# A list-scheduled attention and FFN kernel: a re-tuned scheduler, another order of loads, and zero matmuls while PE waits for q

## The chip, the cores and the metric

The kernel runs on one core of one Trainium2 chip. The metric is the device time of one execution in microseconds (us), as the median over several runs. The core has a tensor engine (PE, with its weight loads shown apart as PEld), a vector engine (DVE), a scalar engine (ACT), POOL and SP. In this kernel POOL issues the loads of q, k, v and the weights from HBM, and SP issues the transposing DMAs and the stores. The program gives each engine its own instructions in a fixed order, and in these traces one that waits holds up what stands behind it on the same engine: while one copy on DVE waited 8.9 us (profile after), DVE did nothing else.

## The reference

Block-sparse attention over 4 batches, 8 heads, 768 positions and head size 64 is followed by a multiplicative FFN of 3072 tokens.

```python
scores = scale * np.matmul(q, k.transpose(0, 1, 3, 2))
# mask: neighbouring 32-blocks, first and last block, 3 sampled blocks per row
scores = np.where(mask, scores, -1000000000.0)
attn = softmax(scores)
x = (attn @ v)            # reordered to (3072, 512)
a = x @ w1                # 512 -> 1024
b = x @ w2
h = a * b @ w3            # (a * b) @ w3
out = h @ w_out           # 1024 -> 512
```

## The kernel before

The kernel folds w3 @ w_out into one matrix (wf). It computes all scores densely, exponentiates them on ACT (144 tiles of 128x1024), multiplies by a 0/1 mask on DVE, and multiplies by v on PE. The FFN of 512 tokens at a time is woven in between. The order on every engine comes from a list scheduler that runs while the program is built. It is a small model of the chip: each task has a cost per engine, and a task that depends on another may start when the scheduler thinks the other's result is *seen*.

```python
SEEN = {"PE": 0.22, "ACT": 0.10, "DVE": 0.10, "POOL": 0.12, "SP": 0.05}
SWITCH = 0.095
...
    t.end = start + t.costs[eng]
    t.seen = t.end + t.flight + SEEN[eng]      # commit()
...
    for d in t.deps:                           # run(): earliest start of a task
        e = d.seen
        base = max(base, e)
...
    elif t.kind == "xbar":                     # a transposing DMA
        xbar = max(xbar, t.end + 1.6) + t.bytes / 250e3
        t.seen = xbar + 0.4
...
def pick_pe(self, cands, free, mode):
    soon = [c for c in cands if c[0] <= max(t0, now) + 0.06]
    if mode == "S":                            # PE has just done a score tile
        s = [c for c in soon if c[1].mode == "S"]
        if s:
            return min(s, ...)                 # stay with score tiles
```

A score tile is four matmuls that use 64 of the 128 rows of PE, two heads side by side (`s[:, h, ...]`, 64x128 weights). All other matmuls use 128 rows, and the scheduler charges `SWITCH` for a change between the two kinds. Score tiles are chained, each one depending on the one before it:

```python
ts = add(f"S {sk}", {PE: 0.216}, sc, deps=QK[b, pr] + [prev_s], writes=[sk], ..., mode="S")
prev_s = ts
```

There are two PSUM buffers for score tiles. q and k of batch 0 are transposed on PE. Those of batches 1 to 3 are rearranged on DVE (`qs`, three buffers) and transposed by a DMA into `qkt` (eight buffers).

The softmax here doesn't subtract the row's maximum and nothing guards it: scores larger than these inputs give would overflow.

Of the kernel before, what the change touches and what calls it, by code (L numbers as in the profile page):

```python
# [18 lines left out]

class Task:  # L20
    def __init__(self, name, costs, deps, writes, reads, go, kind, prio, mode, flight):
        self.name, self.costs, self.deps = name, costs, deps
        self.writes, self.reads, self.go = writes, reads, go
        self.kind, self.prio, self.mode, self.flight = kind, prio, mode, flight
        self.end = None
        self.seen = None


class Plan:
# [12 lines left out]
    def add(self, name, costs, go, deps=(), writes=(), reads=(), kind="", prio=0, mode="N", flight=0.0):  # L42
        t = Task(name, costs, [d for d in deps if d is not None], list(writes), list(reads), go,
                 kind, prio, mode, flight)
        for key in set(t.writes) | set(t.reads):
            self.users[key] += 1
# [34 lines left out]
    def run(self):  # L81
# [13 lines left out]
        while ready:  # L95
            best = None
            ests = defaultdict(list)
            for t in ready:
# [4 lines left out]
                for d in t.deps:  # L103
                    e = d.seen
                    base = max(base, e)
                t.base = base
                for eng, cost in t.costs.items():
                    ests[eng].append((max(base, free[eng]), t))
# [12 lines left out]
            if len(t.costs) > 1:  # L121

                opts = []
                for e2, cost in t.costs.items():
                    opts.append((max(t.base, free[e2]) + cost + self.bias.get(e2, 0.0), e2))
                e2 = min(opts)[1]
                if e2 != eng:
                    eng, start = e2, max(t.base, free[e2])
# [6 lines left out]
            if t.kind == "load":  # L135
                lane = max(lane, t.end + 1.6) + t.bytes / 350e3
                t.seen = lane + 0.15
                for key in t.writes:
                    self.freed[key] = t.seen
            elif t.kind == "xbar":  # L140
                xbar = max(xbar, t.end + 1.6) + t.bytes / 250e3
                t.seen = xbar + 0.4
# [17 lines left out]
    bias = {}  # L160

    def pick(self, eng, cands, free):
        t0 = min(c[0] for c in cands)
        near = [c for c in cands if c[0] <= t0 + 0.12]
        return min(near, key=lambda c: (c[1].prio, c[0]))

    def pick_pe(self, cands, free, mode):
        now = free["PE"]
        t0 = min(c[0] for c in cands)
        soon = [c for c in cands if c[0] <= max(t0, now) + 0.06]  # L170
# [12 lines left out]
    def feed(self, s, free):  # L183

        held = self.slots["s"]
        busy = sum(1 for k in held[-self.bufs["s"]:] if self.left[k] or self.freed[k] > free["PE"] + 0.25)
# [8 lines left out]
def kernel(  # L195
# [36 lines left out]
        "w3n": ([128, d_ff], BF16, 4, None),  # L232
        "w3t": ([128, NF, 128], BF16, 3, None),
        "e": ([128, 2, 512], BF16, 8, None),
        "rec": ([128, 2, 2, 1], F32, 2, None),
        "xn": ([128, 2, d_model], BF16, 3, None),
        "x": ([128, 4, 512], BF16, 4, None),
# [4 lines left out]
        "o": ([128, 2, 2, D + 1], F32, 1, PSUM),  # L242
        "f": ([128, 512], F32, 3, PSUM),
# [100 lines left out]
    load_pair(0, 1, "qk")  # L344
    load_pair(0, 0, "v")
    load_pair(0, 1, "v")
    load_wo(0)
    load_wo(1)
    load_w3(0)
    load_w3(1)  # L350
    load_pair(0, 2, "qkv")
    load_w3(2)
    load_w3(3)
    load_pair(0, 3, "qkv")
    for i in range(4, NF):
        load_w3(i)
    for c in range(4):
        load_w12("w1", moe_w1, w1_sb, c)
        load_w12("w2", moe_w2, w2_sb, c)
    for b in range(1, B):  # L360
        for pr in range(NP):
            load_pair(b, pr, "qkv")
# [20 lines left out]
    for r in range(3):  # L383
        dst = Ab if r == 2 else A
        prev = dve(f"R{r}", 0.17, [prev, t_rf], lambda r=r, dst=dst: V.scalar_tensor_tensor(
            dst, in0=JJ, scalar=rand_f[:, r:r + 1], in1=A, op0=ALU.is_equal, op1=ALU.max))
    t_Ab = prev
    t_hot0 = dve("hot0", 0.6, [t_hotf], lambda: V.tensor_scalar(
        hot, in0=hotf, scalar1=0.0, scalar2=None, op0=ALU.is_ge))
    t_hot = dve("hot", 0.75, [t_hot0], lambda: V.scalar_tensor_tensor(  # L390
# [4 lines left out]
    for i, (lo, n) in enumerate(((0, 512), (512, 256))):  # L395
# [5 lines left out]
            t, G[:, lo:lo + n], T(*key)[:NB, :n]), deps=[m], reads=[key], prio=0))  # L401
    t_mask = {}
    for t3 in range(NT):
        for kp in range(3):
            key = ("f", "M", t3, kp)

            def mm(t, key=key, t3=t3, kp=kp):
# [4 lines left out]
            m = add(f"mask {t3} {kp}", {PE: 0.22}, mm, deps=g, writes=[key], prio=2.5)  # L412
            t_mask[t3, kp] = add(f"mask {t3} {kp} c", both(0.58, 0.69), lambda t, key=key, t3=t3, kp=kp: copy_on(
                t, mask[:, t3, kp, :], T(*key)), deps=[m], reads=[key], prio=1)
# [4 lines left out]
    def prepare(b, pr):  # L419
        done = []  # L420
        for x, tag in ((0, "qn"), (1, "kn")):
            src = (tag, b, pr)
            dst = ("qkt", b, pr)
            if b == 0:
                key = ("f", "qk", b, pr, x)

                def tr(t, key=key, src=src):
# [7 lines left out]
                done.append(add(f"tc {b}{pr}{x}", both(0.81, 0.5), lambda t, key=key, dst=dst, x=x: copy_on(  # L435
                    t, T(*dst)[:, x, :], T(*key, shape=[128, S], dt=BF16)), deps=[m], writes=[dst],
                    reads=[key], prio=0))
            else:
                mid = ("qs", b, pr, x)
                m = add(f"re {b}{pr}{x}", {DVE: 0.45}, lambda t, mid=mid, src=src: nc.vector.tensor_copy(  # L440
                    T(*mid), T(*src).rearrange("p h c d -> p c h d")), deps=[LD[src]], writes=[mid],
                    reads=[src], prio=4)
                t = add(f"xb {b}{pr}{x}", {SP: 0.3}, lambda t, mid=mid, dst=dst, x=x: nc.sync.dma_start(
# [12 lines left out]
        V1[b, pr] = add(f"v1 {b}{pr}", {DVE: 0.6}, widen, deps=[LD[src]], writes=[dst], reads=[src],  # L456
# [8 lines left out]
    for b in range(B):  # L465
        if b == 0:
            units += [(b, t, 2 * Q + i) for Q in range(2) for t in range(NT) for i in range(2)]
        else:
            units += [(b, t, pr) for t in range(NT) for pr in range(NP)]
# [3 lines left out]
    for b, t3, pr in units:  # L473
        chain = None
        for kp in range(3):
            sk, ek, qk = ("s", b, t3, pr, kp), ("e", b, t3, pr, kp), ("qkt", b, pr)

            def sc(t, sk=sk, qk=qk, t3=t3, kp=kp):
# [12 lines left out]
                T(*ek), T(*sk), AF.Exp, scale=1.0 / 8.0), deps=[ts], reads=[sk], writes=[ek], prio=2)  # L491
            tm = add(f"K {ek}", {DVE: 0.70}, lambda t, ek=ek, t3=t3, kp=kp: nc.vector.tensor_tensor(  # L492
                T(*ek), T(*ek), mask[:, t3, kp:kp + 1, :].to_broadcast((128, 2, 512)), op=ALU.mult),
                deps=[te, t_mask[t3, kp]], writes=[ek], prio=2)
# [3 lines left out]
            def va(t, ek=ek, ok=ok, b=b, pr=pr, kp=kp):  # L498
                e, o, w = T(*ek), T(*ok), T("v1", b, pr)
                for k2 in range(2):  # L500
                    kc = 2 * kp + k2
                    for qt in range(2):
# [6 lines left out]
                        reads=[ek, ("v1", b, pr)], kind="value", prio=1.5)  # L509
# [3 lines left out]
        tr = add(f"rec {rk}", {DVE: 0.15}, lambda t, rk=rk, ok=ok: nc.vector.reciprocal(  # L513
            T(*rk), T(*ok)[:, :, :, D:]), deps=[chain], reads=[ok], writes=[rk], prio=0)
        tx = add(f"xn {rk}", {DVE: 0.40}, lambda t, rk=rk, ok=ok, xk=xk, pr=pr: nc.vector.tensor_tensor(  # L515
# [129 lines left out]
```

## Time and profile before

The three runs took 297.84, 297.88 and 300.91 us (median 297.88). The profiled execution took 296.79 us.

Lines from the page of the profile before. First come busy time, share of the span and number of instructions by engine. Then follow the tenths of PE's busy time in 40 slices of 7.4 us, the granted clock of PE in the same slices, and the chain of work that ended last as shares of the span.

```profile
span 295.0 us, 6214 instructions
...
PE 256.7 (87%) x2505; PEld 121.0 (41%) x2548; DVE 185.4 (63%) x396; ACT 184.6 (63%) x221; POOL 46.2 (16%) x75
...
PE   2989999768689995699999999799999999948994
...
PEclk9999999997959997999999999999999999995998
...
PE 69%; DMA 18%; ACT 4%; DVE 4%; issue 3%; SPq 1%; POOL 0%; DVEq 0%; ACTq 0%; POOLq 0%
PE f L576 26%; PE s L483 13%; DMA qkt<-qs 13%; PE o L505 12%; PE f L595 11%; ACT e L490 4%; PE f L557 4%; DMA x<-xn 3%; DVE e L492 2%; DMA kn<-in_k_dram 1%; PE f L431 1%; PE f L409 1%; PE f L545 1%; SPq L528 1%; DVE xn L515 1%
```

The clock row cannot be read at the very start: it shows 9 (90% or more) in the slices up to 20 us, where score tiles take 0.61 us for 0.39 later. The row of tenths shows three holes: near 60 to 85 us, near 115 us and near 265 us. The chain gives 13% of the span to transposing DMAs of q and k. The list of waits shows who stood there. These are DVE between 60 and 125 us, ACT between 120 and 220 us, and PE after 260 us. The columns are engine, tile and line, what it waited for, total us, number of waits and longest wait.

```profile
DVE qs L440 <- DMA qkt<-qs: 20.9, 6, 4.6
...
ACT e L490 <- PE s L483: 22.3, 37, 2.6
...
PE f L576 <- DMA x<-xn: 4.5, 1, 4.5
```

DVE stood 20.9 us at copies into `qs`, whose buffers were still being read by transposes. In the steady stage ACT, which makes the exponentials, waited 37 times for a score tile. Near the end PE waited 4.5 us for the last x. A stretch of PE's timeline from the steady stage (start, length, what, count) shows how the work is laid out:

```profile
157.19 0.59 PE L576 MATMUL f<-x,w 128*128 128x512 bf16 x2
157.72 0.39 PE L483 MATMUL s<-qkt 64*128 64x256 bf16 x4
158.04 0.61 PE L576 MATMUL f<-x,w 128*128 128x512 bf16 x2
158.48 0.41 PE L505 MATMUL o<-v,e 128*128 128x65 bf16 x8
```

The lengths overlap (the pair at 158.04 takes 0.61 us, and the next group starts 0.44 us later), so one reads *starts*. In long back-to-back runs an FFN matmul starts every 0.216 us, so the pair that starts at 157.19 has its slots used up at 157.62. The score tile starts 0.10 us later. It starts at 157.72 and the next kind at 158.04: 0.32 us for a tile that costs 0.22 when another follows it (shown below). Every stretch of score matmuls thus costs about 0.2 us beside its work. This place is typical: over the 58 one-tile stretches between 120 and 218 us the median from first start to next kind is 0.325 us. The built program has 137 such stretches for 144 tiles.

I use **PE work**: the number of weight loads of each kind, times the start-to-start interval of that kind in back-to-back stretches (0.216 us for a 512-column matmul, 0.22 for a score tile, 0.24 for eight value matmuls). Narrower matmuls count for less.

### The profile page before, as it was taken

Reading aid. Unit: us, or ns where it says so; the run is one execution under the profiler, and the core shown is the slowest. Engines: PE = TensorE matmul, PEld = TensorE weight load, DVE = VectorE, ACT = ScalarE, POOL = GpSimd, SP = SyncE. Lnnn points to the kernel's source line nnn. Section 1 sums busy time; section 2 is a strip of 40 time slices with the busy share of each in tenths; the row PEclk is TensorE's granted clock in tenths of the full one; section 3 lists DMA queues with packets and bytes.
Section 4 is the critical chain, followed back from the end, with each engine's and each line's share of the span. In section 5 each row is a group of like instructions: output and inputs, shape, how many; then the busy total and the mean of one; then the engine's idle time right before and its main releaser. Section 6 shows DMA issues by size and latency. Waiting matters only on the chain.

```text
span 295.0 us, 6214 instructions
## 1 busy us (share of the span) xinstructions
PE 256.7 (87%) x2505; PEld 121.0 (41%) x2548; DVE 185.4 (63%) x396; ACT 184.6 (63%) x221; POOL 46.2 (16%) x75
## 2 busy tenths in 40 slices
PE   2989999768689995699999999799999999948994
PEld 1455545532234432244444444444443444422441
DVE  4578887943457853688777666867756776640331
ACT  2598896814546673477677767968777777730320
POOL 8634452042122232001000000000000000000000
PEclk9999999997959997999999999999999999995998
DMA  6999999699989999936750101301014001130003
GB/s 81 165 206 207 209 203 198 105 131 156 139 128 137 122 171 188 151 70 111 126 154 1 29 10 73 107 2 20 18 38 129 17 2 36 54 109 18 0 2 142
DMA packets 52193, 29.25 MB, mean 99 GB/s; under 512 B 33732, under 2 KB 47044, under 8 KB 52164
## 3 DMA queue, kind: packets, MB, share of 16 engines
q0 software_dynamic: 16416, 14.68, 34.8%
q1 hardware_dynamic: 35748, 14.16, 25.1%
q8 instruction: 20, 0.33, 0.4%
q14 instruction: 9, 0.07, 0.1%
HBM read 29.36 MB, written 6.29 MB: 121 GB/s over the span
## 4 chain that ended last, share of the span: by engine, by line
PE 69%; DMA 18%; ACT 4%; DVE 4%; issue 3%; SPq 1%; POOL 0%; DVEq 0%; ACTq 0%; POOLq 0%
PE f L576 26%; PE s L483 13%; DMA qkt<-qs 13%; PE o L505 12%; PE f L595 11%; ACT e L490 4%; PE f L557 4%; DMA x<-xn 3%; DVE e L492 2%; DMA kn<-in_k_dram 1%; PE f L431 1%; PE f L409 1%; PE f L545 1%; SPq L528 1%; DVE xn L515 1%
## 5 line engine op out<-in xcount | busy, mean ns | idle before, releaser
L490 ACT ACTIVATE e<-s 128x1024 bf16<-128x1024 f32 x144 | 144.5, 1026 | 58.1 <-PE s L483 52.2
L576 PE MATMUL f<-x,w 128*128 128x512 bf16 x361 | 103.7, 402 | 9.5 <-DMA x<-xn 5.3
L492 DVE TENSOR_TENSOR e<-e,mask 128x1024 bf16<-128x1024 bf16 x144 | 96.7, 686 | 18.4 <-ACT e L490 17.9
L505 PE MATMUL o<-v,e 128*128 128x65 bf16 x1152 | 60.3, 197 | 8.2 <-DVE e L492 4.1
L505 PEld LDWEIGHTS <-e 128*128 128x128 bf16 x1152 | 50.4, 99 | 41.7 <-issue 9.9
L483 PE MATMUL s<-qkt 64*128 64x256 bf16 x576 | 58.7, 283 | 9.2 <-DMA qkt<-qs 4.6
L587 DVE TENSOR_TENSOR h<-f,a 128x512 bf16<-128x512 f32 x48 | 33.0, 688 | 30.8 <-PE f L576 20.0
L595 PE MATMUL f<-wf,h 128*128 128x512 bf16 x180 | 48.8, 380 | 1.2 <-issue 1.0
L576 PEld LDWEIGHTS <-w 128*128 128x128 bf16 x384 | 31.1, 101 | 41.8 <-issue 17.7
L584 ACT CAST a<-f 128x512 bf16<-128x512 f32 x48 | 28.0, 583 | 26.6 <-PE f L576 25.6
L483 PEld LDWEIGHTS <-qkt 64*128 64x128 bf16 x576 | 17.7, 95 | 56.1 <-issue 47.3
L515 DVE TENSOR_TENSOR xn<-o,rec 128x256 bf16<-128x256 f32 x48 | 20.4, 424 | 1.6
L595 PEld LDWEIGHTS <-h 128*128 128x128 bf16 x192 | 14.8, 98 | 15.4 <-issue 5.3
L513 DVE RECIPROCAL rec<-o 128x4 f32<-128x4 f32 x48 | 8.6, 179 | 14.4 <-PE o L505 14.1
L557 PE MATMUL f<-wo,w3t 128*128 128x512 bf16 x56 | 16.6, 381 | 0.5 <-issue 0.2
L300 POOL DMA_DIRECT2D vn<-in_v_dram x16 | 11.6, 725 | 31.2 <-DVE h L587 15.0
L300 POOL DMA_DIRECT2D kn<-in_k_dram x16 | 11.6, 722 | 30.6 <-DVE qs L440 24.5
L300 POOL DMA_DIRECT2D qn<-in_q_dram x16 | 11.8, 739 | 18.1 <-DVE qs L440 9.6
L440 DVE COPY qs<-kn 128x768 bf16<-128x768 bf16 x12 | 4.3, 355 | 16.3 <-DMA qkt<-qs 16.3
L266 DVE COPY ob<-f 128x512 f32<-128x512 f32 x11 | 7.6, 690 | 8.3 <-PE f L595 8.3
L266 ACT COPY ob<-f 128x512 f32<-128x512 f32 x13 | 7.6, 584 | 7.4 <-PE f L595 7.0
L440 DVE COPY qs<-qn 128x768 bf16<-128x768 bf16 x12 | 4.4, 366 | 4.6 <-DMA qkt<-qs 4.6
(48 smaller groups left out, 77.9 us busy)
## 6 DMA issues: line engine op xcount, KB each, us to landing
out_dram<-ob SPq DMA_DIRECT2D x24, 256.0 KB, 2.1
qn<-in_q_dram POOLq DMA_DIRECT2D x16, 192.0 KB, 8.1
kn<-in_k_dram POOLq DMA_DIRECT2D x16, 192.0 KB, 7.7
vn<-in_v_dram POOLq DMA_DIRECT2D x16, 192.0 KB, 6.0
w3n<-in_moe_w_dram POOLq DMA_DIRECT2D x8, 256.0 KB, 9.9
w<-in_moe_w_dram POOLq DMA_DIRECT2D x8, 256.0 KB, 8.9
wo<-in_moe_w_out_dram POOLq DMA_DIRECT2D x2, 512.0 KB, 9.2
qkt<-qs SPq DMA_TRANSPOSE x24, 6.1
```

Of the source, the lines that this page charges most:

```text
L266: (nc.scalar.copy if t.eng == ACT else nc.vector.tensor_copy)(out, in_)
L300: t = add(name, {POOL: 0.73}, lambda t: nc.gpsimd.dma_start(out=out_of(), in_=src), deps=deps, writes=writes, kind="load", prio=seq[0])
L483: nc.tensor.matmul(s[:, h, k2 * QT:(k2 + 1) * QT], lhsT=z[64 * h:64 * h + 64, 1, kc * 128:(kc + 1) * 128], rhs=z[64 * h:64 * h + 64, 0, t3 ...
L490: te = add(f"E {ek}", {ACT: 0.97}, lambda t, sk=sk, ek=ek: nc.scalar.activation(T(*ek), T(*sk), AF.Exp, scale=1.0 / 8.0), deps=[ts], reads ...
L492: tm = add(f"K {ek}", {DVE: 0.70}, lambda t, ek=ek, t3=t3, kp=kp: nc.vector.tensor_tensor(T(*ek), T(*ek), mask[:, t3, kp:kp + 1, :].to_bro ...
L505: nc.tensor.matmul(o[:, qt, h, :], lhsT=e[:, h, lo:lo + 128], rhs=w[:, h, kc, :], start=kc == 0 and qt == 0 and h == 0, stop=kc == C - 1, ...
L515: tx = add(f"xn {rk}", {DVE: 0.40}, lambda t, rk=rk, ok=ok, xk=xk, pr=pr: nc.vector.tensor_tensor(T(*xk)[:, :, 128 * pr:128 * pr + 128].re ...
L557: nc.tensor.matmul(T(*key), lhsT=T("w3t", i)[:, j, :], rhs=wo_sb[:, j, :], start=j == 0, stop=j == NF - 1)
L576: nc.tensor.matmul(T(*key), lhsT=w[:, c, f * 128:(f + 1) * 128], rhs=T(*xk)[:, c, :], start=c == 0, stop=c == 3)
L584: ta = add(f"a {i}{f}", {ACT: 0.58}, lambda t, ak=ak, key=ends["w1"][0]: nc.scalar.copy(T(*ak), T(*key)), deps=[ends["w1"][1]], reads=[end ...
L587: nc.vector.tensor_tensor(T(*hk)[:, f, :], T(*key), T(*ak), op=ALU.mult),
L595: nc.tensor.matmul(T(*key), lhsT=T(*hk)[:, f, n * 128:(n + 1) * 128], rhs=wf_sb[:, f, :], start=f == 0, stop=f == NF - 1)
```

## The change

Its stated intent is a list schedule with score tiles in pairs, loads in the order w3, batch 1, w1, w2, and zero matmuls on PE while it waits for q. The arithmetic stays as it was. The core of the diff, with cuts:

```diff
+LOADS = ("a01 v00 a02 v01 a03 v02 v03 o0 o1 30 31 32 33 34 35 36 37 "
+         "p10 p11 p12 p13 10 20 11 21 12 22 13 23 "
+         "p20 p21 p22 p23 p30 p31 p32 p33")
+WARM = 8
+PRM = dict(bias=0.4, bmask0=1.0, ..., eprio=0.5, aprio=1.0, ...)
+LONG = ("load", "xbar", "store")
@@ run(): earliest start
-                for d in t.deps:
-                    e = d.seen
-                    base = max(base, e)
-                t.base = base
-                for eng, cost in t.costs.items():
-                    ests[eng].append((max(base, free[eng]), t))
+                for eng in t.costs:
+                    at = base
+                    for d in t.deps:
+                        at = max(at, d.end if d.eng == eng and not d.flight and d.kind not in LONG else d.seen)
+                    t.base[eng] = max(at, free[eng])
+                eng = min(t.costs, key=lambda e: t.base[e] + t.costs[e] + t.bias.get(e, 0.0))
+                ests[eng].append((t.base[eng], t))
@@ transposing DMAs
-                xbar = max(xbar, t.end + 1.6) + t.bytes / 250e3
-                t.seen = xbar + 0.4
+                xbar = max(xbar, t.end + 0.6) + t.bytes / 250e3
+                t.seen = max(xbar + 0.4, t.end + (4.0 if lane > t.end else 1.2))
@@ buffers
-        "w3n": ([128, d_ff], BF16, 4, None),
+        "w3n": ([128, d_ff], BF16, 8, None),
-        "x": ([128, 4, 512], BF16, 4, None),
+        "x": ([128, 4, 512], BF16, 3, None),
@@ zero matmuls
+    for i in range(WARM):
+        add(f"warm {i}", {PE: 0.427}, lambda t: nc.tensor.matmul(
+            T("f", "warm"), lhsT=zero[:, :128], rhs=zero, start=True, stop=True), ...)
@@ SP cost of a transpose / of a store
-{SP: 0.3} ... {SP: 0.1}
+{SP: 1.25} ... {SP: 0.55}
@@ units of batch 0: all four head pairs for one query tile, then the next tile
-            units += [(b, t, 2 * Q + i) for Q in range(2) for t in range(NT) for i in range(2)]
+        units += [(b, t, pr) for t in range(NT) for pr in range(NP)]
```

(The rest: costs of small tasks nearer to the measured ones, and biases and priorities for tasks that ACT or DVE could do.)

More of the change, by code (lines that the diff above doesn't have):

```diff
@@ L17 @@
 SWITCH = 0.095
+LOADS = ("a01 v00 a02 v01 a03 v02 v03 o0 o1 30 31 32 33 34 35 36 37 "
+         "p10 p11 p12 p13 10 20 11 21 12 22 13 23 "
+         "p20 p21 p22 p23 p30 p31 p32 p33")
+WARM = 8
+PRM = dict(bias=0.4, bmask0=1.0, bmask=1.0, btc=0.5, near=0.12, soon=0.06, kprio=2.0, eprio=0.5, aprio=1.0,
+           hprio=1.0, vprio=1.5, w3prio=10.0, ebufs=8, both=0.25, fo="31", pcopy=4.0)
+LONG = ("load", "xbar", "store")
 class Task:
@@ L26, in __init__ @@
         self.seen = None
+        self.base = {}
 class Plan:
@@ L40, in __init__, with add @@
         self.pool_of = {}
-    def add(self, name, costs, go, deps=(), writes=(), reads=(), kind="", prio=0, mode="N", flight=0.0):
+    def add(self, name, costs, go, deps=(), writes=(), reads=(), kind="", prio=0, mode="N", flight=0.0, bias=None):
         t = Task(name, costs, [d for d in deps if d is not None], list(writes), list(reads), go,
                  kind, prio, mode, flight)
+        t.bias = {"DVE": PRM["bias"]} if bias is None else bias
         for key in set(t.writes) | set(t.reads):
@@ L120, in run @@
             start, eng, t = picks[0]
-            if len(t.costs) > 1:
-                opts = []
-                for e2, cost in t.costs.items():
-                    opts.append((max(t.base, free[e2]) + cost + self.bias.get(e2, 0.0), e2))
-                e2 = min(opts)[1]
-                if e2 != eng:
-                    eng, start = e2, max(t.base, free[e2])
             if eng == "PE":
@@ L135, in run @@
             if t.kind == "load":
-                lane = max(lane, t.end + 1.6) + t.bytes / 350e3
-                t.seen = lane + 0.15
+                lane = max(lane, t.end + 1.75) + t.bytes / 375e3
+                t.seen = lane + 0.2
                 for key in t.writes:
@@ L158, in run @@
         return self.log
-    bias = {}
     def pick(self, eng, cands, free):
         t0 = min(c[0] for c in cands)
-        near = [c for c in cands if c[0] <= t0 + 0.12]
+        near = [c for c in cands if c[0] <= t0 + PRM["near"]]
         return min(near, key=lambda c: (c[1].prio, c[0]))
@@ L169, in pick_pe @@
         t0 = min(c[0] for c in cands)
-        soon = [c for c in cands if c[0] <= max(t0, now) + 0.06]
+        soon = [c for c in cands if c[0] <= max(t0, now) + PRM["soon"]]
         if mode == "S":
@@ L185, in feed @@
         held = self.slots["s"]
-        busy = sum(1 for k in held[-self.bufs["s"]:] if self.left[k] or self.freed[k] > free["PE"] + 0.25)
+        busy = sum(1 for k in held[-self.bufs["s"]:] if self.left[k] or self.freed[k] > free["PE"] + PRM["both"])
         if self.bufs["s"] - busy >= 2:
@@ L231 @@
         "qkt": ([128, 2, S], BF16, 8, None),
-        "w3n": ([128, d_ff], BF16, 4, None),
+        "w3n": ([128, d_ff], BF16, 8, None),
         "w3t": ([128, NF, 128], BF16, 3, None),
-        "e": ([128, 2, 512], BF16, 8, None),
+        "e": ([128, 2, 512], BF16, PRM["ebufs"], None),
         "rec": ([128, 2, 2, 1], F32, 2, None),
         "xn": ([128, 2, d_model], BF16, 3, None),
-        "x": ([128, 4, 512], BF16, 4, None),
+        "x": ([128, 4, 512], BF16, 3, None),
         "h": ([128, NF, 512], BF16, 2, None),
@@ L241 @@
         "s": ([128, 2, 512], F32, 2, PSUM),
-        "o": ([128, 2, 2, D + 1], F32, 1, PSUM),
-        "f": ([128, 512], F32, 3, PSUM),
+        "o": ([128, 2, 2, D + 1], F32, int(PRM["fo"][1]), PSUM),
+        "f": ([128, 512], F32, int(PRM["fo"][0]), PSUM),
     }
@@ L343 @@
     t_hotf = iota("hotf", hotf, 0.82, pattern=[[1, C], [C, 128]], base=0, channel_multiplier=-BLK)
-    load_pair(0, 1, "qk")
-    load_pair(0, 0, "v")
-    load_pair(0, 1, "v")
-    load_wo(0)
-    load_wo(1)
-    load_w3(0)
-    load_w3(1)
-    load_pair(0, 2, "qkv")
-    load_w3(2)
-    load_w3(3)
-    load_pair(0, 3, "qkv")
-    for i in range(4, NF):
-        load_w3(i)
-    for c in range(4):
-        load_w12("w1", moe_w1, w1_sb, c)
-        load_w12("w2", moe_w2, w2_sb, c)
-    for b in range(1, B):
-        for pr in range(NP):
-            load_pair(b, pr, "qkv")
+    for item in LOADS.split():
+        kind, rest = item[0], item[1:]
+        if kind == "o":
+            load_wo(int(rest))
+        elif kind == "3":
+            load_w3(int(rest))
+        elif kind in "12":
+            load_w12("w" + kind, moe_w1 if kind == "1" else moe_w2, w1_sb if kind == "1" else w2_sb, int(rest))
+        else:
+            load_pair(int(rest[0]), int(rest[1]), {"a": "qk", "v": "v", "p": "qkv"}[kind])
+    zero = fixed("zero", [128, 512], BF16)
+    t_zero = add("zero", {DVE: 0.2}, lambda t: nc.vector.memset(zero, 0.0), prio=-1)
+    for i in range(WARM):
+        add(f"warm {i}", {PE: 0.427}, lambda t: nc.tensor.matmul(
+            T("f", "warm"), lhsT=zero[:, :128], rhs=zero, start=True, stop=True),
+            deps=[t_zero], writes=[("f", "warm")], prio=-1)
     def dve(name, cost, deps, go, **kw):
@@ L384 @@
         dst = Ab if r == 2 else A
-        prev = dve(f"R{r}", 0.17, [prev, t_rf], lambda r=r, dst=dst: V.scalar_tensor_tensor(
+        prev = dve(f"R{r}", 0.23, [prev, t_rf], lambda r=r, dst=dst: V.scalar_tensor_tensor(
             dst, in0=JJ, scalar=rand_f[:, r:r + 1], in1=A, op0=ALU.is_equal, op1=ALU.max))
     t_Ab = prev
-    t_hot0 = dve("hot0", 0.6, [t_hotf], lambda: V.tensor_scalar(
+    t_hot0 = dve("hot0", 0.55, [t_hotf], lambda: V.tensor_scalar(
         hot, in0=hotf, scalar1=0.0, scalar2=None, op0=ALU.is_ge))
-    t_hot = dve("hot", 0.75, [t_hot0], lambda: V.scalar_tensor_tensor(
+    t_hot = dve("hot", 0.94, [t_hot0], lambda: V.scalar_tensor_tensor(
         hot, in0=hotf, scalar=float(BLK), in1=hot, op0=ALU.is_lt, op1=ALU.mult))
@@ L400 @@
         t_G.append(add(f"G{i}c", both(0.6, 0.6), lambda t, key=key, lo=lo, n=n: copy_on(
-            t, G[:, lo:lo + n], T(*key)[:NB, :n]), deps=[m], reads=[key], prio=0))
+            t, G[:, lo:lo + n], T(*key)[:NB, :n]), deps=[m], reads=[key], prio=0, bias={}))
     t_mask = {}
@@ L411 @@
             g = [t_G[0]] if t3 < 2 else [t_G[1]]
-            m = add(f"mask {t3} {kp}", {PE: 0.22}, mm, deps=g, writes=[key], prio=2.5)
+            m = add(f"mask {t3} {kp}", {PE: 0.22}, mm, deps=g, writes=[key], prio=1.2 if t3 == 0 else 5 + t3)
             t_mask[t3, kp] = add(f"mask {t3} {kp} c", both(0.58, 0.69), lambda t, key=key, t3=t3, kp=kp: copy_on(
-                t, mask[:, t3, kp, :], T(*key)), deps=[m], reads=[key], prio=1)
+                t, mask[:, t3, kp, :], T(*key)), deps=[m], reads=[key], prio=1 if t3 == 0 else 3,
+                bias={ACT: PRM["bmask0"] if t3 == 0 else PRM["bmask"]})
     QK, V1 = {}, {}
@@ L434, in prepare @@
                         prio=1)
-                done.append(add(f"tc {b}{pr}{x}", both(0.81, 0.5), lambda t, key=key, dst=dst, x=x: copy_on(
+                done.append(add(f"tc {b}{pr}{x}", both(0.81, 0.56), lambda t, key=key, dst=dst, x=x: copy_on(
                     t, T(*dst)[:, x, :], T(*key, shape=[128, S], dt=BF16)), deps=[m], writes=[dst],
-                    reads=[key], prio=0))
+                    reads=[key], prio=0, bias={ACT: -0.3 * x if pr == 0 else PRM["btc"]}))
             else:
                 mid = ("qs", b, pr, x)
-                m = add(f"re {b}{pr}{x}", {DVE: 0.45}, lambda t, mid=mid, src=src: nc.vector.tensor_copy(
+                m = add(f"re {b}{pr}{x}", {DVE: 0.37}, lambda t, mid=mid, src=src: nc.vector.tensor_copy(
                     T(*mid), T(*src).rearrange("p h c d -> p c h d")), deps=[LD[src]], writes=[mid],
                     reads=[src], prio=4)
-                t = add(f"xb {b}{pr}{x}", {SP: 0.3}, lambda t, mid=mid, dst=dst, x=x: nc.sync.dma_start(
+                t = add(f"xb {b}{pr}{x}", {SP: 1.25}, lambda t, mid=mid, dst=dst, x=x: nc.sync.dma_start(
                     out=T(*dst)[:, x, :].rearrange("p (c n) -> p c n", c=C),
@@ L455, in widen @@
             nc.vector.tensor_copy(w[:, :, :, :D], T(*src))
-        V1[b, pr] = add(f"v1 {b}{pr}", {DVE: 0.6}, widen, deps=[LD[src]], writes=[dst], reads=[src],
+        V1[b, pr] = add(f"v1 {b}{pr}", {DVE: 0.42}, widen, deps=[LD[src]], writes=[dst], reads=[src],
                         prio=3 if b == 0 else 4)
@@ L465 @@
     for b in range(B):
-        if b == 0:
-            units += [(b, t, 2 * Q + i) for Q in range(2) for t in range(NT) for i in range(2)]
-        else:
-            units += [(b, t, pr) for t in range(NT) for pr in range(NP)]
+        units += [(b, t, pr) for t in range(NT) for pr in range(NP)]
     Xdone = defaultdict(list)
@@ L490 @@
             te = add(f"E {ek}", {ACT: 0.97}, lambda t, sk=sk, ek=ek: nc.scalar.activation(
-                T(*ek), T(*sk), AF.Exp, scale=1.0 / 8.0), deps=[ts], reads=[sk], writes=[ek], prio=2)
+                T(*ek), T(*sk), AF.Exp, scale=1.0 / 8.0), deps=[ts], reads=[sk], writes=[ek], prio=PRM["eprio"])
             tm = add(f"K {ek}", {DVE: 0.70}, lambda t, ek=ek, t3=t3, kp=kp: nc.vector.tensor_tensor(
                 T(*ek), T(*ek), mask[:, t3, kp:kp + 1, :].to_broadcast((128, 2, 512)), op=ALU.mult),
-                deps=[te, t_mask[t3, kp]], writes=[ek], prio=2)
+                deps=[te, t_mask[t3, kp]], writes=[ek], prio=PRM["kprio"])
             ok = ("o", b, t3, pr)
@@ L508 @@
             chain = add(f"V {ek}", {PE: 0.24}, va, deps=[tm, V1[b, pr], prev_v], writes=[ok],
-                        reads=[ek, ("v1", b, pr)], kind="value", prio=1.5)
+                        reads=[ek, ("v1", b, pr)], kind="value", prio=PRM["vprio"])
             prev_v = chain
@@ L512 @@
         rk, xk = ("rec", b, t3, pr), ("xn", b, t3)
-        tr = add(f"rec {rk}", {DVE: 0.15}, lambda t, rk=rk, ok=ok: nc.vector.reciprocal(
+        tr = add(f"rec {rk}", {DVE: 0.17}, lambda t, rk=rk, ok=ok: nc.vector.reciprocal(
             T(*rk), T(*ok)[:, :, :, D:]), deps=[chain], reads=[ok], writes=[rk], prio=0)
-        tx = add(f"xn {rk}", {DVE: 0.40}, lambda t, rk=rk, ok=ok, xk=xk, pr=pr: nc.vector.tensor_tensor(
+        tx = add(f"xn {rk}", {DVE: 0.42}, lambda t, rk=rk, ok=ok, xk=xk, pr=pr: nc.vector.tensor_tensor(
             T(*xk)[:, :, 128 * pr:128 * pr + 128].rearrange("p t (h d) -> p t h d", h=2),
@@ L527 @@
             for qt in range(2):
-                t = add(f"xx {b}{t3}{qt}", {SP: 0.3}, lambda t, xk=xk, i=i, half=half, qt=qt: nc.sync.dma_start(
+                t = add(f"xx {b}{t3}{qt}", {SP: 1.25}, lambda t, xk=xk, i=i, half=half, qt=qt: nc.sync.dma_start(
                     out=T("x", i)[:, :, half * QT + qt * 128:half * QT + qt * 128 + 128],
@@ L584 @@
             ta = add(f"a {i}{f}", {ACT: 0.58}, lambda t, ak=ak, key=ends["w1"][0]: nc.scalar.copy(
-                T(*ak), T(*key)), deps=[ends["w1"][1]], reads=[ends["w1"][0]], writes=[ak], prio=1)
+                T(*ak), T(*key)), deps=[ends["w1"][1]], reads=[ends["w1"][0]], writes=[ak], prio=PRM["aprio"])
             hs.append(add(f"h {i}{f}", {DVE: 0.69}, lambda t, ak=ak, key=ends["w2"][0], hk=hk, f=f:
                           nc.vector.tensor_tensor(T(*hk)[:, f, :], T(*key), T(*ak), op=ALU.mult),
-                          deps=[ta, ends["w2"][1]], reads=[ends["w2"][0], ak], writes=[hk], prio=1))
+                          deps=[ta, ends["w2"][1]], reads=[ends["w2"][0], ak], writes=[hk], prio=PRM["hprio"]))
         for n in range(4):
@@ L603 @@
             b, c = divmod(4 * i + n, C)
-            add(f"st {i}{n}", {SP: 0.1}, lambda t, bk=bk, b=b, c=c: nc.sync.dma_start(out=outv[b, c], in_=T(*bk)),
+            add(f"st {i}{n}", {SP: 0.55}, lambda t, bk=bk, b=b, c=c: nc.sync.dma_start(out=outv[b, c], in_=T(*bk)),
                 deps=[tb], reads=[bk], kind="store", prio=2)
```

## The prediction

> **What bounds the kernel now.** The page's PE busy (256.7 of 295.0 us) averages four stages. I count PE work from weight loads in ten-us windows, at the issue intervals of back-to-back stretches of the timeline (128x512 matmul 0.216 us, score tile 0.22, eight value matmuls 0.24): about 214 us.
> - 0 to 60 us: 37 us of work: attention of batch 0, held by ACT (36 exponentials of 1.03 us plus copies), and w3 times w_out. PE is cold until about 20 us: four score matmuls take 0.61 us before, 0.39 after.
> - 60 to 120: 36 us of work. In the list of waits DVE stands 20.9 us at q/k rearranging copies until a transpose DMA has freed their buffer (landing 6.1 us median). Its queue is in order, so masks, h products and later loads wait behind (POOL 24.5 us). ACT waits 21.1 us for scores; the clock falls to 0.83. The chain has transposes of 9.4, 10.7, 8.5 and 9.3 us here, 13% of the span.
> - 120 to 260: near saturation, 8.4 to 9.0 us of work per 10 (the rest is switching between matmul kinds).
> - 260 to 295: 4.5 us waiting for the last x, a cold restart, one FFN tile.
>
> **What changes.** Same arithmetic. Added: a memset and eight 128x512 zero matmuls in PE's first 4.8 idle us. The rest is order: batch 1 loads before w1/w2, eight w3 buffers for four, batch 0 by query tile so that x completes earlier, three x buffers for four, and above all a schedule that counts 1.25 us on SP and 4 us of latency for a transpose under load (before: 0.3 and about 2), so that copies stand where their buffers are really free.
>
> **Cost, on the critical path.**
> 1. Start: the Trainium skill, "TensorE: Matmul & The Clock Gate", Part 1, says the clock starts at half rate and rises after about 3.4 us of activity; 0.61 against 0.39 us agrees. About 9 us of cold PE work lie on the chain before 20 us; I expect 2 to 4 us back, since ACT and DMA bound this stage too.
> 2. 60 to 120: at 8.8 per 10 it would do 53 us of work, not 36. Batch 1's q/k can be transposed during batch 0 (eight qkt buffers hold two batches). Transposes will still land later than assumed, so I count 14 to 18 us, with new DVE waits at 35 to 55 us.
> 3. The stall before the last x and its restart: 0 to 4 us.
> 4. 120 to 260: 0 to 4 us from better pairing.
>
> Sum 20 to 30 us, less some slip: **269 us, range 259 to 281**. Faster by over 2%: 0.93; within 2%: 0.05; slower: 0.02. Saturation from 20 us on would give about 262.
>
> **What would show it.** (1) Score groups near 0.4 us before 15 us; ten or more exponentials by 20 us (before: 6). (2) DVE's wait for transposes under 8 us; 60 to 120 us holds some 36 exponentials (before: 23), clock above 0.95; transposes under 4% of the chain. (3) Busy time per instruction unchanged within 2%. (4) 120 us to the end gains less than the middle.
>
> **What would make it wrong.** Transposes delayed by loads could stall DVE during batch 0 instead, moving the gap to 40 to 60 us. w1/w2 come last: if they land after 60 us PE starves, as three x buffers bound how far attention runs ahead. A new order could lose pairing in the steady stage, or leave two FFN tiles for the tail. The zero matmuls could stop too early, so that PE cools before the first transposes.

## More of the kernel before

The whole kernel is about 214.5 us of work. Counted in windows of ten us the sums are good to 1 to 3 us: a recount from each single weight load, with narrow matmuls in proportion to their columns, gives 215.5 us.

## The result, and the profile after

Four runs took 265.81, 265.90, 266.49 and 273.13 us, median 266.19. The last is marked slow. Here the mark goes by the time alone (over 1.5% above the fastest): the granted clock was 0.969 in that run and 0.947 to 0.948 in the three fast ones. The ratio of the fast runs is 0.897 (95% interval 0.886 to 0.908). Ratios in this text are the mean time of one kernel's fast runs over that of the other's of the same rounds, so not quite the ratio of the medians quoted.

The same lines of the page after:

```profile
span 264.1 us, 6276 instructions
...
PE 243.5 (92%) x2516; PEld 129.5 (49%) x2556; DVE 174.8 (66%) x381; ACT 189.5 (72%) x237; POOL 45.9 (17%) x75
...
PE   6888998099899999999999999999999999999993
...
PEclk9655799869999999999999999999999999999999
...
PE 84%; DMA 7%; ACT 3%; issue 3%; POOL 1%; DVE 0%; POOLq 0%; DVEq 0%; ACTq 0%
PE f L577 32%; PE f L596 16%; PE s L484 15%; PE o L506 15%; DMA qkt<-qs 5%; PE f L558 3%; ACT e L491 2%; DMA qn<-in_q_dram 2%; PE f L435 2%; PE f L412 2%; PE f L546 1%; ACT wf L271 0%; POOL qn L305 0%; DVE qs L444 0%; POOL kn L305 0%
```

The late holes are gone. The clock row is low (5 to 7 tenths) from 7 to 33 us, of which more below. An early one has come, a slice of "0" from 46 to 53 us (slices are 6.6 us here). The waits between 20 and 60 us name it (DVE, PE and ACT, the longest of each). The last line is ACT between 120 and 220 us:

```profile
DVE qs L444 <- DMA qkt<-qs: 8.9, 1, 8.9
...
PE o L506 <- DVE v L458: 6.8, 1, 6.8
...
ACT e L491 <- PE s L484: 10.9, 5, 7.4
...
ACT e L491 <- PE s L484: 5.1, 11, 0.8
```

The first transposes of batch 1 are issued at 37.8 us, while the eight 256 KB loads of w1 and w2 are going out. The chain shows 13.5 us until the first has landed. DVE stands 8.9 us, PE 6.8 us behind it, and ACT 7.4 us behind PE. In the steady stage the ACT waits for scores fall from 22.3 to 5.1 us. PE's timeline shows why:

```profile
150.98 0.59 PE L577 MATMUL f<-x,w 128*128 128x512 bf16 x2
151.51 0.61 PE L484 MATMUL s<-qkt 64*128 64x256 bf16 x8
152.05 0.60 PE L577 MATMUL f<-x,w 128*128 128x512 bf16 x2
152.49 0.41 PE L506 MATMUL o<-v,e 128*128 128x65 bf16 x8
```

Score tiles come two at a time (x8). The stretch takes 0.54 us from start to next start (median 0.543 over 37 such stretches), against 0.32 for one tile, so the second tile costs 0.22 and brings no switch. The 0.10 us ahead of the stretch is as before. The built program has 76 score stretches, against 137. At about 0.2 us each, 61 fewer make some 12 us, an estimate from these starts.

Where the time came from, as the moment at which PE had done a given amount of work:

| | 37 us of work | 73 us | 175 us | end of span |
|---|---|---|---|---|
| before | 60 us | 120 | 240 | 295.0 |
| after | 70 | 110 | 220 | 264.1 |
| time for this part, before | 60 | 60 | 120 | 55 |
| time for this part, after | 70 | 40 | 110 | 44 |

The first part lost 10 us, the second gained 20, the third 10 and the last 11. The borders are soft, because 73 us falls into the hole of the kernel before at 110 to 118 us: the recount gives 9 lost, then 16, 13 and 11 gained. Attention now ends sooner (the last score matmul starts at 219.3 us, against 259.9). So the last two FFN tiles follow each other without a wait for x, at 10 us of work per 10 us.

### The profile page after: what moved, and what is told of

The parts are those of the page before. It is cut to its first block, busy times and chain, and to the rows that moved or that the text cites. A ratio compares the mean times of both kernels' runs of the same rounds, so it can differ in the third digit from the quotient of the medians.

```text
span 264.1 us, 6276 instructions
## 1 busy us (share of the span) xinstructions
PE 243.5 (92%) x2516; PEld 129.5 (49%) x2556; DVE 174.8 (66%) x381; ACT 189.5 (72%) x237; POOL 45.9 (17%) x75
## 4 chain that ended last, share of the span: by engine, by line
PE 84%; DMA 7%; ACT 3%; issue 3%; POOL 1%; DVE 0%; POOLq 0%; DVEq 0%; ACTq 0%
PE f L577 32%; PE f L596 16%; PE s L484 15%; PE o L506 15%; DMA qkt<-qs 5%; PE f L558 3%; ACT e L491 2%; DMA qn<-in_q_dram 2%; PE f L435 2%; PE f L412 2%; PE f L546 1%; ACT wf L271 0%; POOL qn L305 0%; DVE qs L444 0%; POOL kn L305 0%
## 5 line engine op out<-in xcount | busy, mean ns | idle before, releaser
L491 ACT ACTIVATE e<-s 128x1024 bf16<-128x1024 f32 x144 | 139.9, 1026 | 23.9 <-PE s L484 22.7
L493 DVE TENSOR_TENSOR e<-e,mask 128x1024 bf16<-128x1024 bf16 x144 | 94.0, 684 | 6.3 <-ACT e L491 6.1
L577 PE MATMUL f<-x,w 128*128 128x512 bf16 x361 | 93.2, 379 | 2.4 <-issue 1.3
L506 PE MATMUL o<-v,e 128*128 128x65 bf16 x1152 | 57.8, 198 | 6.9 <-DVE v L458 6.8
L484 PE MATMUL s<-qkt 64*128 64x256 bf16 x576 | 47.8, 283 | 2.1 <-ACT e L491 1.6
L596 PE MATMUL f<-wf,h 128*128 128x512 bf16 x180 | 46.2, 379 | 0.8 <-issue 0.3
L484 PEld LDWEIGHTS <-qkt 64*128 64x128 bf16 x576 | 22.6, 95 | 30.9 <-issue 26.8
L271 ACT COPY ob<-f 128x512 f32<-128x512 f32 x21 | 12.3, 587 | 13.1 <-PE f L596 11.9
L305 POOL DMA_DIRECT2D qn<-in_q_dram x16 | 11.6, 725 | 33.2 <-DVE qs L444 22.9
L305 POOL DMA_DIRECT2D vn<-in_v_dram x16 | 11.6, 723 | 27.9 <-DVE xn L516 19.0
L558 PEld LDWEIGHTS <-w3t 128*128 128x128 bf16 x64 | 5.8, 100 | 7.2 <-issue 1.5
L271 ACT CAST wf<-f 128x512 bf16<-128x512 f32 x8 | 4.7, 587 | 4.3 <-PE f L558 4.2
```

What stands on the lines that cost most here:

```text
L271: (nc.scalar.copy if t.eng == ACT else nc.vector.tensor_copy)(out, in_)
L305: t = add(name, {POOL: 0.73}, lambda t: nc.gpsimd.dma_start(out=out_of(), in_=src), deps=deps, writes=writes, kind="load", prio=seq[0])
L484: nc.tensor.matmul(s[:, h, k2 * QT:(k2 + 1) * QT], lhsT=z[64 * h:64 * h + 64, 1, kc * 128:(kc + 1) * 128], rhs=z[64 * h:64 * h + 64, 0, t3 ...
L491: te = add(f"E {ek}", {ACT: 0.97}, lambda t, sk=sk, ek=ek: nc.scalar.activation(T(*ek), T(*sk), AF.Exp, scale=1.0 / 8.0), deps=[ts], reads ...
L493: tm = add(f"K {ek}", {DVE: 0.70}, lambda t, ek=ek, t3=t3, kp=kp: nc.vector.tensor_tensor(T(*ek), T(*ek), mask[:, t3, kp:kp + 1, :].to_bro ...
L506: nc.tensor.matmul(o[:, qt, h, :], lhsT=e[:, h, lo:lo + 128], rhs=w[:, h, kc, :], start=kc == 0 and qt == 0 and h == 0, stop=kc == C - 1, ...
```

## The experiments

Two theories were tested first. **A**: the score tiles in pairs are the cause. **B**: the other parts are the cause, meaning the estimates for transposes, the order of loads and the zero matmuls. The prediction had put nearly all of the gain on B.

### b_pair: the kernel before with pairing alone

Nothing in the diff speaks of pairs of score tiles. The line that does it is the new earliest start. Before, a score tile could follow the previous one only 0.22 us after its end (`SEEN["PE"]`), because it depends on it. That is outside the window of 0.06 us in which the scheduler looks for the next task, so it nearly always took something else in between (137 stretches for 144 tiles). PE needs no such delay between two of its own tasks: the second tile of a pair starts at once in the profile after.

```diff
-                    e = d.seen
+                    e = d.end if t.kind == "score" and d.kind == "score" else d.seen
```

> The kernel before with one change: in the list scheduler a score tile counts the previous score tile as done at its end, not 0.22 us later. The built program has 79 stretches of score matmuls on PE for 137. Theory A (pairing is what made the steady stage faster: about 0.1 us for each switch saved, and score tiles ready earlier for ACT): 287 to 293 us, 9.1 or more us of PE work per 10 us after 120 us, against 8.8. Theory B (pairing is a side effect; the gain comes from the other parts): 296 to 299 us. If pairing also lets attention run ahead, the stall of 4.5 us before the last x goes too.

Measured: **265.2 us** (264.1 to 265.44, four fast runs), ratio 0.894 (0.886 to 0.902). This one line gives the whole gain, and far more than theory A had expected. (The record's automatic verdict is "unclear" for all runs on this chip, b_pair, a_nopair, a_tiny and a_xbarold, and for b_late and b_early, without a reason given. The times of b_pair and of the kernel before, 294.42 to 301.31 us here, lie far apart.) PE's tenths on its page:

```profile
PE   1989999949389999999999999999999999999993
```

DVE's longest waits in it between 60 and 125 us that end with a DMA:

```profile
DVE qs L440 <- DMA vn<-in_v_dram: 5.1, 1, 5.1
DVE qs L440 <- DMA qkt<-qs: 3.2, 3, 2.3
```

DVE's wait for transposes fell from 20.9 to 3.2 us, although nothing about transposes was changed. The hole at 115 us is gone, and that near 50 to 75 us remains. The last score matmul starts at 225.0 us, and PE has no wait from 220 us on.

### a_nopair: the kernel after without pairing

```diff
-    at = max(at, d.end if d.eng == eng and ... else d.seen)
+    at = max(at, d.seen if t.kind == 'score' and d.kind == 'score' else d.end if d.eng == eng and ... else d.seen)
```

> The kernel after with only that one estimate put back (133 stretches of score matmuls for 76). Theory A: 272 to 280 us, with the steady rate back at about 8.8 per 10 and the wait before the last x back. Theory B: 265 to 268 us.

Measured: 293.47 us (292.95 to 294.4), ratio to before 0.989 (0.982 to 0.997). Theory A had expected 272 to 280. All the rest of the change together, without pairing, is worth 1.1%. Added to pairing it shows nothing: 0.897 against 0.894, with intervals that overlap.

### b_late and b_early: pairing in half of the batches

```diff
+ ... if t.kind == "score" and d.kind == "score" and t.writes[0][1] >= 2 else d.seen   # b_late
+ ... if t.kind == "score" and d.kind == "score" and t.writes[0][1] < 2 else d.seen    # b_early
```

> The kernel before with the pairing estimate for the score tiles of batches 2 and 3 alone (104 stretches of score matmuls for 137; all batches: 79). Theory A (a stretch costs PE about 0.2 us, so the gain follows the number of stretches saved in stages where PE is the bound, and attention that runs ahead ends the wait for the last x): steady stage from about 150 us and the tail gain 15 to 20 us, so 278 to 283 us, while 60 to 120 us stays as before. Theory B (the gain of pairing comes from the middle stage, where another order happened to end the transposes' waits): 290 us or more.

> The same for the score tiles of batches 0 and 1 alone (114 stretches). Theory A: the gain of the middle stage alone, 10 to 14 us, so 284 to 288 us; the wait for the last x is back. Theory B: 270 us or less.

Measured: b_late 279.34 us, ratio 0.942 (0.936 to 0.948); b_early 278.61 us, ratio 0.940 (0.935 to 0.946). b_late is within theory A's range. b_early gained more than A had said. In the same table of moments:

| | stretches | 37 us of work | 73 | 175 | end of span |
|---|---|---|---|---|---|
| before | 137 | 60 | 120 | 240 | 295.0 |
| b_late | 104 | 61 | 119 | 232 | 278.2 |
| b_early | 114 | 61 | 108 | 224 | 276.2 |
| b_pair | 79 | 61 | 107 | 217 | 262.3 |
| after | 76 | 70 | 110 | 220 | 264.1 |
| a_nopair | 133 | 70 | 124 | 243 | 292.1 |

Pairing in the late batches leaves the middle as it was (119 against 120). It gains 7 us in the steady part (113 us for 120) and 9 in the tail (46 for 55). Pairing in the early ones gains 12 us by 73 us of work, then 4 and then 3. The two spans fall by 16.8 and 18.8 us, 35.6 in sum, against 32.7 for both together. So the gain is nearly additive over the stages: it comes neither from the middle alone nor from the steady stage and tail alone. The steady rate follows the pairs: by the recount, PE did 9.3 us of work per 10 from 160 to 220 us in b_late, where tiles come in pairs there, against 8.5 in b_early and 8.4 in the kernel before, where they do not.

### a_tiny and a_tiny5 with a_again: the zero matmuls

The zero matmuls were cut from 512 to 8 columns. The order on every engine stays the same.

```diff
-            T("f", "warm"), lhsT=zero[:, :128], rhs=zero, ...
+            T("f", "warm")[:, :8], lhsT=zero[:, :128], rhs=zero[:, :8], ...
```

> The kernel after, same order of instructions on every engine, with the eight zero matmuls 8 columns wide for 512. Theory A (the zero matmuls end before the real work and PE is cold again by 9 us, so they are worth nothing): 266 us within 0.5%. Theory B (they are worth the 2 to 4 us of the prediction): 268 to 270 us.

The first four runs took 265.95, 268.3, 269.9 and 272.2 us (the last one slow), which fits neither theory well. So both kernels went to a chip together:

> The kernel after, unchanged, beside the next run on one chip, because the first run of the small zero matmuls scattered from 265.9 to 272.2 us. All theories: 265.5 to 267 us in most runs, now and then about 273.

> The zero matmuls 8 columns wide again, five rounds beside the kernel after. Theory A (they are worth nothing): the medians of the two differ by less than 1.5 us, and the scatter is as in the other. Theory B (they are worth 2 to 4 us): this one is slower by 2 us or more in the median, and its profile shows fewer score tiles done by 20 us.

Measured: the kernel after took 265.79 us once and 272.24 to 275.47 us five times, all five slow. a_tiny5 took 269.12 to 270.95 us in five fast runs and 273.25 in a slow one. With one fast run against five the comparison stays unclear. In the fast runs a_tiny's kernel is 2 to 5 us slower; over all ten runs of each the means are 270.5 us (after) and 270.1 us (8 columns). Whether the zero matmuls are worth anything is left open. So is why the kernel after took 272 us or more in six of its ten runs. The profiles, though, show what the zero matmuls do. First the start of the kernel after, then that of a_tiny (PE's timeline):

```profile
1.19 3.59 PE L363 MATMUL f<-zero 128*128 128x512 bf16 x8 [1.19 <-DVE zero L361]
4.77 0.85 PE L435 MATMUL f<-ident,qn 128*64 128x128 bf16 x12
6.42 0.53 PE L435 MATMUL f<-ident,kn 128*64 128x128 bf16 x12 [0.80 <-DMA kn<-in_k_dram]
6.88 0.49 PE L400 MATMUL f<-hot,Ab 24*24 24x512 bf16 x2
7.84 0.61 PE L484 MATMUL s<-qkt 64*128 64x256 bf16 x8 [0.48 <-ACT qkt L271]
9.11 0.77 PE L435 MATMUL f<-ident,qn 128*64 128x128 bf16 x12 [0.66 <-DMA qn<-in_q_dram]
...
23.77 1.50 PE L506 MATMUL o<-v,e 128*128 128x65 bf16 x24
...
28.99 0.61 PE L484 MATMUL s<-qkt 64*128 64x256 bf16 x4
```

```profile
4.87 0.85 PE L435 MATMUL f<-ident,qn 128*64 128x128 bf16 x12 [3.30 <-DMA qn<-in_q_dram]
6.24 0.85 PE L435 MATMUL f<-ident,kn 128*64 128x128 bf16 x12 [0.52 <-DMA kn<-in_k_dram]
7.02 0.81 PE L400 MATMUL f<-hot,Ab 24*24 24x512 bf16 x2
7.99 1.03 PE L484 MATMUL s<-qkt 64*128 64x256 bf16 x8 [0.15 <-ACT qkt L271]
8.95 0.85 PE L435 MATMUL f<-ident,qn 128*64 128x128 bf16 x12
```

With full zero matmuls the transposes of k take 0.53 us instead of 0.85, and two score tiles 0.61 instead of 1.03. The clock does rise at about 6.4 us. From 9.1 us the groups take the cold lengths again (0.77), and 24 value matmuls at 23.8 us still take 1.50 us, against 0.98 for the same group at 29.5 us. The warmth lasts about 3 us, in a stage where PE waits for loads. After 60 us the two have done the same work, 29.3 and 29.8 us.

What matters more: the kernel after stays cold *longer* than the kernel before, whose score tiles are at the warm length from 20.6 us on:

```profile
20.62 0.40 PE L483 MATMUL s<-qkt 64*128 64x256 bf16 x4
```

In the kernel after one still takes 0.61 us at 28.99 us. From 20 to 30 us PE was busy 9.4 us in it and 9.6 in the kernel before, but did 5.1 and about 8.3 us of work (recount). So about 3 of the 10 us that the first part lost went here, and most of the rest in and around the stall at 46 to 53 us. a_tiny is as cold (1.50 us for the value matmuls at 23.68 us), so it is not due to the zero matmuls. With the old order of loads (a_loadold, below) transposes are back at 0.53 us from 24.1 us.

### a_xbarold and b_pairxbar: the estimates for transposes and DMA issue

a_xbarold puts the old estimates into the kernel after. b_pairxbar puts the new ones into the kernel before with pairing.

```diff
# a_xbarold (b_pairxbar is the reverse)
-                xbar = max(xbar, t.end + 0.6) + t.bytes / 250e3
-                t.seen = max(xbar + 0.4, t.end + (4.0 if lane > t.end else 1.2))
+                xbar = max(xbar, t.end + 1.6) + t.bytes / 250e3
+                t.seen = xbar + 0.4
-{SP: 1.25} ... {SP: 0.55}
+{SP: 0.3} ... {SP: 0.1}
```

> The kernel after with the old estimates for DMA issue and transposes (0.3 us on SP for 1.25, 0.1 for 0.55, about 2 us of latency for 4). Theory A (these estimates ended the waits of 60 to 120 us): 275 us or more, DVE waiting 15 us or more for transposes. Theory B (it is the order of loads, batch 1 before w1 and w2, that lets the middle stage run; the estimate of 4 us is wrong by so much that it hardly matters): within 2% of 266 us.

> The kernel before with pairing and with the new estimates for transposes and DMA issue. In the kernel after the old estimates cost 14 us. Theory A (the new ones are better in themselves): 258 to 263 us. Theory B (what an estimate is worth hangs on the order that it happens to give; 4 us is still far below the 6 to 17 us seen): between 263 and 275 us, no gain on the 265.2 of pairing alone.

Measured: a_xbarold 280.38 us (279.52 to 283.58), ratio 0.947; b_pairxbar 269.23 us (266.93 to 270.71), ratio 0.906 (0.899 to 0.912). Taking the new estimates out of the kernel after costs 14 us. Putting them into the kernel before with pairing gains nothing: it was 4 us slower than b_pair in the median, though on another chip, and the intervals of the two ratios overlap. Theory A of a_xbarold had the time right but not its reason: DVE waited 8.6 us for transposes there, not 15 or more. Undoing a part of a jointly tuned set therefore told how well the set fits together, not what that part is worth. Neither estimate is near the truth. The transposes of q and k took 2.7 to 17.3 us to land in the kernel after (median 6.4).

### a_loadold: the old order of loads

```diff
-LOADS = ("a01 v00 a02 v01 a03 v02 v03 o0 o1 30 ... 37 p10 p11 p12 p13 10 20 ... 23 ...
+LOADS = ("a01 v00 v01 o0 o1 30 31 p02 32 33 p03 34 ... 37 10 20 ... 23 p10 p11 p12 p13 ...
```

> The kernel after with the order of loads of before (w1 and w2 ahead of batch 1). Theory A (batch 1 ahead of w1 and w2 puts its transposes among eight 256 KB weight loads and so makes the stall at 40 to 52 us): 262 to 267 us with no wait of DVE over 5 us before 55 us. Theory B (the order helps, as the prediction had it): 272 us or more.

Measured: 272.07 us (271.37 to 272.55, all fast), ratio 0.916 (0.911 to 0.920). The stall at 45 us is gone (31.4 us of work done by 50 us, against 24.4), so theory A was right about where the order of loads puts the stall. But PE does only 5.0, 4.8 and 2.7 us of work in the tens from 70, 80 and 100 us. The time is 272, as theory B had it. The order moves the stall and does not remove it.

### b_pairpe1 and a_pe1: q and k of batch 1 transposed on PE

This was an attempt at a faster version. It removes the eight transposing DMAs of batch 1, of which three stand on the chain of b_pair for 21.9 us between 58 and 85 us.

```diff
-            if b == 0:          # in prepare(): transpose on PE
+            if b <= 1:
```

> The kernel before with pairing for all batches, and q and k of batch 1 transposed on PE as those of batch 0 are, so that eight of 24 transpose DMAs under load fall away. Theory A (the 50 to 80 us stage, which does 16 us of PE work in 30, waits for these transposes and for nothing else): 254 to 260 us, 7 or more us of PE work in each ten from 50 to 80. Theory B (that stage is held by when the loads of batch 1 arrive, and the transposes only stand last in the queue): 262 to 266 us.

> The kernel after with the same change for batch 1. Theory A: 255 to 262 us, the wait of DVE near 40 us (8.9 us) gone, and no runs of 272 us and more, because those are runs in which transposes landed later still. Theory B: as the kernel after, 266 or 273 us.

Measured: b_pairpe1 **277.25 us**, ratio 0.933, that is 12 us *slower* than b_pair. a_pe1 took 265.99 and 267.63 us in fast runs and 271.19 and 272.8 in slow ones, ratio 0.898, no change, as its theory B had said. Both theories missed for b_pairpe1. The hole at its place was filled: 7.2 and 9.6 us of work in the tens from 50 and 70 us, where b_pair had 4.9 and 5.5. It came back later: 2.2 us of work from 100 to 110 us and 4.7 from 110 to 120, where b_pair had 9.5 and 9.2. These are PE's waits of b_pairpe1 between 90 and 120 us:

```profile
PE o L505 <- DVE xn L515: 5.1, 2, 4.6
PE f L576 <- DMA x<-xn: 4.8, 1, 4.8
```

In this program SP issues no transpose of q and k from 46 to 84.7 us. Its queue holds six transposes of x, and those of batch 2 follow only after them, with 13 us for six. By 120 us it has done 77.8 us of work, b_pair 85.3. Another order of the same work moved the stall to the next batch. Why the scheduler's new order held batch 2 back was not tried out.

### What the middle stage shows

By 120 us the programs had done 73.4 us of work (before), 70.7 (a_nopair), 70.5 (a_xbarold), 77.3 (a_loadold), 77.8 (b_pairpe1), 78.8 (b_pairxbar), 82.6 (after), 84.7 (b_early) and 85.3 (b_pair). Every edit of the scheduler, whatever it was meant for, makes a new order on all engines, and the time lost in this stage changes with it (b_pairpe1 took 12 us more than b_pair in all). That pairing *leads to* a good order here is shown by b_early and b_pair. By which single wait it does so stays open, since no run changed the order of one queue alone. Nor did a run change the order at random without pairs, so how much of the gain in this stage any other order would have brought is not shown. No version was clearly faster than the kernel after in its fast runs. b_pair equals it with one line, and none of its four runs was slow, against six of ten of the kernel after. These runs were on different chips.

## Why the prediction was right or wrong

The time (269 against 266.2 us measured, range 259 to 281) was right. Its reasons mostly were not, and their errors cancelled: the four steps were to bring 2 to 4, 14 to 18, 0 to 4 and 0 to 4 us, and brought about -10 (with the stall at 46 us), 20, 11 and 10. That the sum came out near is luck.

- **"1. Start ... I expect 2 to 4 us back"**: wrong in kind. The zero matmuls do warm PE, for about 3 us, but then PE stayed cold until about 29 us, 8 us longer than before. Score tiles still took 0.61 us at 11.6 us (said: near 0.4 before 15 us), eight exponentials were done by 20 us, not ten, and with or without warm-up PE has done the same work by 60 us. The first part of the kernel became 10 us *slower*.
- **"2. 60 to 120 ... I count 14 to 18 us, with new DVE waits at 35 to 55 us"**: the size (20 us for the same work) was near, and the warning about DVE came true exactly: 8.9 us at 42 to 51 us. But 10 of the 20 us only pay back what the cold start and the early stall took. And the cause named, "above all a schedule that counts ... 4 us of latency for a transpose under load", is not the cause: without pairing, all of that is worth 1.1% (a_nopair). Of the signs, DVE's wait for transposes fell to 9.3 us (said: under 8), the transposes' share of the chain to 5% (said: under 4%), 60 to 120 us holds 47 exponentials (said: 36), and the clock there is 1.00 (said: above 0.95).
- **"3. The stall before the last x and its restart: 0 to 4 us"**: mis-sized. The tail gained 11 us. The wait went away because attention ended 40 us sooner, and two FFN tiles then ran without switches. The prediction had listed two tiles in the tail as a danger.
- **"4. 120 to 260: 0 to 4 us from better pairing"**: the step that failed. I put pairing last and at 0 to 4 us. It is worth 10 us in the steady part, most of the tail, and about 12 us before it, 32 us in all (b_pair). Only some 12 of these are switches saved, by the estimate above; the rest, by subtraction, came with the order that pairs led to. I had read the words "in pairs" but had not looked for the line that makes pairs, nor counted the score stretches (137), nor priced one from the timeline (0.2 us). All of this could have been read beforehand.
- **"120 us to the end gains less than the middle"**: wrong. In the moments table the net gain up to 73 us of work is 10 us, and after it 21 us.

## What to carry to other kernels

When a scheduler writes the program, look for the dependency that it prices wrongly before tuning its costs. One 0.22 us latency charged between two tasks of the same in-order engine cost this kernel 32 us: it all but forbade pairs, and with them went the switches saved (an estimated 12 us) and an order in which attention ends sooner. Price the switches between kinds of matmul by start-to-start times, not by busy time. Do not take a new order's gain in one stage for the effect of the edit that made it. When a large diff wins, run each part alone on the old kernel as well as taken out of the new one: taking one part out cost 14 us here, and the same part put into the other kernel gained nothing.

## What the Trainium skill lacked or had wrong

- "TensorEngine Tiling (Array Packing)", Key Properties, says that changing the tiling mode drains the TensorE, and gives no figure. Here a change between 64-row score matmuls and 128-row matmuls cost about 0.10 us each way (starts at 157.62 to 157.72 and 158.04 above), 0.2 us for a stretch. 61 fewer stretches are an estimated 12 us.
- "TensorE: Matmul & The Clock Gate", Part 1, says that about 3.4 us of activity raises the clock, and that an idle window lowers it. This agrees at the start: eight zero matmuls over 3.6 us, after which groups fell from 0.85 to 0.53 us. It gives no share of activity that holds the clock or raises it again: PE was cold again by 9.1 us, with gaps of no more than 0.8 us listed between its groups and 2.2 busy us in the 4.1 from 5 to 9.1 us, and it stayed so until about 29 us, although it was busy 9.8 of the 10.9 us from 9.1 to 20 us and 9.4 of the next 10. Which of the small matmuls there (transposes, masks on 24 rows, score tiles on 64) count as activity was not tested.
- "DMA: Bandwidth & Descriptors", DMA Transpose (X-bar), has no figure for the latency of a transpose beside bulk loads. One of 192 KB landed in 2.7 us at best and 17.3 us at worst in the kernel after.
